# Rows for the maxima cleared ahead of a group's transfers, value sums behind the hash bits, and six lists of a hand-written order

## The chip, the core and the metric

The program runs on one core of a Trainium2 chip. TensorE (PE) multiplies, VectorE (DVE), ScalarE (ACT) and GpSimd (POOL) work element by element, and SyncE (SP) issues most of the transfers. Each engine takes its own instructions strictly in order and waits on semaphores for the others. The metric is the time of one launch in microseconds (us); lower is better.

## What is computed

Inputs are q, k and v of 4 batches, 8 heads, 768 rows of 64, and a projection of 64 to 6. Attention is masked by hash buckets, and a routed two-layer network follows (its part is not touched here and is cut):

```
q_bits = (einsum('bhsd,dk->bhsk', q, proj) > 0);  k_bits likewise
mask   = q_bucket[:, :, :, None] == k_bucket[:, :, None, :]
scores = where(mask, scale * q @ k.T, -1e9)
attn   = exp(scores - max);  attn = attn / (sum(attn) + 1e-9)
x      = attn @ v, heads side by side      # 3072 tokens of 512
out    = the token's expert: relu(x @ w1[e]) @ w2[e]
```

## The kernel before

The 32 heads are worked in 8 groups G of 4 heads (j = 0 to 3). Each group's operands lie in tiles QA, KA, QB, KB, VH, VL, WF, of which there are two copies, taken in turn (u = G%2). The partitions of QA are shared out: 0 to 63 hold q in half precision, 64 to 69 the six signs of its hash bits, and 96 to 127 a row block for the negated row maximum, which must be zero while the maximum itself is being found.

Time in the program is counted in steps t, six to a head (one for each 128 keys), and in half-steps n = 2t and 2t+1. In step t of head h, PE makes two halves of the scores transposed (`ST`, L258 and L259, each into one of three PSUM tiles `pst`), one score block for the maximum of a head up to nine steps ahead (`S_pass`, L240, into `pss`), and the products with the values four steps behind (`AV`, L273 to L275, closed by L279 or L280). ACT takes the exponential of each half (L260, `pt`). The rounding rest of `pt`, called `lo` (L263), is made by POOL, or by DVE for the steps named in `XL` and `PAT`: `XL` lists for a head the steps that DVE takes, and a head that is not listed has `PAT`, [5] for an even one and [3] for an odd one (heads 0 and 1 have lists of their own). DVE also reduces each `pss` (L242) to the maximum and divides the finished head by its sum (`norm`, L287 to L290). Heads end as pairs in the transfer to `x_dram` (L293).

A group is prepared while the group ahead of it is worked. All of that is placed by hand: a function is put down for a half-step with `add`, and the tables `P1`, `P2`, `P3` (groups 1 to 3) and `P4` (the later ones, counted from 48(G-1)) give the half-steps. Entries 0 to 7 are the casts of q and k to half precision on ACT (`cast`, L128), 8 to 11 their rests on POOL (`sub`, L130), 12 the hash bits (`bits`: 16 matmuls of 32 columns on PE, L142, a compare on DVE, L143; `bscale` one half-step later), 15 the casts of the values (`cv`, L192) with their rests on POOL (`sv`, L193), and 18 `sumv`: twelve matmuls of 32 columns (L204) that add up the values and a copy to `sq` (L206), followed SW = 4 half-steps later by `sumw` (two matmuls L210, a cast L213, and a DVE instruction L214 that writes WF).

`moves(G)`, at half-step MV, puts the group's operands in place: 22 transfers on SP's queue in one row, among them the rows of qa, qb, ka, kb (L174 to L180), the eight transfers of signs (L172, 9 KB each), and the loads of the next group's q and k (L61, 768 KB each). `clear(G)`, at half-step 48(G-1)+CL, is one transfer of zeros, 192 KB, to partitions 96 to 127 of QA (L191). For group 2, `moves` stands at half-step 59, and `clear` also at 59 (48+11); it is added later and so comes behind it. For the groups behind it, `moves` stands at 96 or 48(G-1)+1, and `clear` ten or eleven half-steps later.

Of the kernel before, what the change touches and what calls it, by code (L numbers as in the profile page):

```python
# [19 lines left out]
AP=dict(PAT=[[5], [3]],  # L20
 E0=[3, 5],
 E1=[3, 4],
 X=[2, 2, 5],
 MR=2,
 LEAD=9,
 S=[7, 7],
 DW=[12, 0, 0, 0, 384],
 P1=[13, 13, 14, 16, 17, 17, 23, 21, 16, 27, 21, 26, 23, 24, 33, 32, 3, 4, 49, -7, 3, 13],
 P2=[41, 44, 48, 49, 51, 51, 57, 55, 45, 49, 55, 57, 52, 60, 59, 61, 2, 3, 75, 32, 36, 47],
 P3=[69, 74, 83, 83, 85, 87, 88, 86, 77, 83, 87, 89, 94, 95, 96, 106, 0, 1, 120, 59, 63, 88],  # L30
 P4=[-33, -34, -25, -21, -13, -5, -9, -5, -18, -12, -3, 0, -5, 7, 10, 10, 3, 4, 36, -55, -50, -11],
 L0=[109, 2],
 EA=[[0, 0], [0, -1], [307, 4]],
 SW=4,
 XL={4: [0, 3, 5], 7: [1], 8: [0, 2, 4], 12: [2, 4, 5], 14: [0, 5], 18: [0, 5], 20: [0, 5], 29: [0, 1, 5], 30: [2]},
 BS=1,
 MV=[27, 59, 96, 1],
 CL=11,
 WS=-23,
 SU=16,  # L40
 OPS='b0 i3 i2 t0 w2 b1 w3 r0 r2 s0 w2 s1 C1 C0 r1 t1 c1 w4 s2 c0 w3 g0 l0 l1 u0 u1 B0 m0 a0 D0 s3 L0 L1 w2 e0 s4 d0 r3 l3 v2 v0 e1 w2 s5 e2 r5 l2 m1 s6 | s7 | x0 | s8 | v1 x1 | s9 | r4 s10 m2 | | s11 v3 f0 | x3 | | x2 m3 | | | | | |')
# [4 lines left out]
def attention(tc, nc, ctx, qT, kT, vv, proj, wg, x_dram, L, jp, identf, B, late=None, after=None):  # L46
# [84 lines left out]
    def bits(G,pairs):  # L131
        if (G,'b') not in TMP: TMP[G,'b']=dp.tile([128,S],F16,name="bt",bufs=1)
        bt=TMP[G,'b']; r=slice(0,128)
        ps=psS.tile([128,2,512],F32,name="pss")
        for hf in range(2):
            if G==0:
                for w in range(2):
                    T.matmul(ps[32*w:32*w+32,hf,0:384],pr,(qd,kd)[w][:,1,hf*384:hf*384+384],start=True,stop=True,tile_position=(0,32*w))
            for p in pairs:
                for w in range(2):  # L140
                    cg=64*p+32*w
                    T.matmul(ps[cg:cg+32,hf,0:384],pr,LD[G][w][:,p,hf*384:hf*384+384],start=True,stop=True,tile_position=(0,cg))  # L142
        V.tensor_scalar(bt.rearrange("p (z q) -> p z q",z=2),ps[:,:,0:384],0.0,0.5,op0=ALU.is_gt,op1=ALU.subtract)  # L143
# [51 lines left out]
    def sumv(G):  # L195
        u=G%2
        if G<2:
            A.copy(WF[u][96:128,:,64],wc[96:128,:].to_broadcast([32,4]))
        ps=psT.tile([128,512],F32,name="pst")
        n=0  # L200
        for c in range(6):
            for src in (VH[u],VL[u]):
                g=32*(n%4)
                T.matmul(ps[g:g+32,0:256].rearrange("p (j d) -> p j d",j=4),on,src[:,:,c,0:64],start=n<4,stop=n>7,skip_group_check=True,tile_position=(0,g)); n+=1  # L204
        SQ[G]=dp.tile([128,256],F32,name="sq",bufs=1)
        A.copy(SQ[G],ps[:,0:256])  # L206
# [54 lines left out]
    def lo(h,kc,eng):  # L261
        p,l=PT[h,kc]
        eng.tensor_tensor(l,p,p.bitcast(BF)[:,1::2],op=ALU.subtract)  # L263
# [18 lines left out]
    def norm(h):  # L282
# [8 lines left out]
        if hh%2:  # L291
            r=slice(64*hh-64,64*hh+64)
            SY.dma_start(x_dram[b*768:(b+1)*768,r].rearrange("(c p) d -> p c d",p=128),X[b][:,:,r])  # L293
    XH,XL=(XT[:,2*i:2*i+2].bitcast(F16).rearrange("p d c q -> p (d c q)").rearrange("p (d c q) -> p d c q",d=4,c=6) for i in range(2))
    def wsplit():
        A.copy(wgs[:,:,0],wgr); G_.tensor_tensor(wgs[:,:,1],wgr,wgs[:,:,0],op=ALU.subtract)
    def xtr(b,d,hf):
# [3 lines left out]
        A.copy(XH[:,d,r],p)  # L301
        V.tensor_tensor(XL[:,d,r],p,XH[:,d,r],op=ALU.subtract)
    LP=[]
    def logits(b,ds):
# [3 lines left out]
        for d in ds:  # L308
            for c in range(6): T.matmul(p[:,c],XH[:,d,c],wgs[:,d],start=(d==0 and c==0),stop=False,skip_group_check=True)
            for c in range(6): T.matmul(p[:,c,0],XL[:,d,c],wgs[:,d,0],start=False,stop=(d==3 and c==5),skip_group_check=True)  # L310
        if ds[-1]==3: V.reduce_sum(L[:,b*6:b*6+6],p.rearrange("p c z e -> p c e z"),axis=AX.X)
# [3 lines left out]
    def add(n,f,*a): at.setdefault(n,[]).append((f,a))  # L315
# [10 lines left out]
    for o in AP['OPS'].split():  # L326
# [2 lines left out]
        else: add(n,OPS[o[0]],int(o[1:]))  # L329
        if o[0]=='e': early.append(int(o[1:]))  # L330
    add(AP['WS'],wsplit); add(AP['SU'],sumv,0); add(AP['SU']+2,sumw,0)
    for G in range(1,NG):
        p=AP['P1'] if G==1 else AP['P2'] if G==2 else AP['P3'] if G==3 else [48*(G-1)+x for x in AP['P4']]
        st,sg=(AP['P4'] if G>3 else p)[16:18]
        for w in range(3):
            if w==2: add(p[19+w],load,G,w)
        for n in range(8): add(p[n],cast,G,n//2%2,n//4,n%2)
        for n in range(4): add(p[8+n],sub,G,n%2,n//2)
        add(p[12],bits,G,[0,1]); add(p[12]+AP['BS'],bscale,G); add(AP['MV'][G-1] if G<4 else 48*(G-1)+AP['MV'][3],moves,G)
        for j in range(4): add(p[15]+st*j,cv,G,j); add(p[15]+st*j+sg,sv,G,j,G_)  # L340
        add(p[18],sumv,G); add(p[18]+AP['SW'],sumw,G)
        if G>1: add(48*(G-1)+AP['CL'],clear,G)

    k=12; done={}; half={}; S_at={}
# [18 lines left out]
    def run(n):  # L363
        for f,a in at.get(n,[]): f(*a)
# [5 lines left out]
    for t in range(6*NH+LAG+6):  # L370
# [7 lines left out]
        if t>=1 and (t-1)//6<NH:  # L378
            hh,ss=divmod(t-1,6)
            lo(hh,ss,V if ss in (E0 if hh<1 else E1 if hh<2 else AP['XL'].get(hh,PAT[hh%2])) or t==6*NH else G_)  # L380
        run(2*t+1)
# [540 lines left out]
@with_exitstack  # L922
def tile_bucket_attention_moe(ctx, tc, qT, kT, vv, proj, wg, w1, w2, out):
    nc = tc.nc
    B = qT.shape[0] // 2
    drp = ctx.enter_context(tc.tile_pool(name="drp", bufs=1, space=DR))
    x_dram = drp.tile([768 * B, 512], F32, name="x_dram")
    M = Moe(tc, nc, ctx, 768 * B)
    late = M.consts()
    with ExitStack() as c1:  # L930
        c1.enter_context(tc.manual_schedule())
        attention(tc, nc, c1, qT, kT, vv, proj, wg, x_dram, M.Lm, M.jp, M.identf, B, late, M.early)
    with ExitStack() as c2:
        M.open(c2, x_dram, w1, w2, out)
        with tc.manual_schedule():
            M.start()
            M.run()
# [34 lines left out]
```

## Time and profile before

| | us |
|---|---|
| median of three runs | 703.8 (703.52 to 705.65) |
| the profiled execution | 706.58 |
| its span in the trace | 704.4 |
| PE busy in the span | 664.3 (94%) |
| POOL, DVE, ACT busy | 517.8, 499.9, 472.1 |

Attention fills the span to about 380 us, the routed network the rest. PE counts as busy from the start of a matmul to its modelled end, so that a stretch with short gaps shows as full; the clock (PEclk) is the share of TensorE's 2.4 GHz that was granted, and 0.50 is its lower level, 1.2 GHz. An "idle before" in square brackets behind a row of the timeline is how long the engine had nothing to do ahead of it, and what released it; "issue" means that the profile shows no engine that did.

### The profile page before, as it was taken

Reading aid. Unit: us, or ns where it says so; the run is one execution under the profiler, and the core shown is the slowest. Engines: PE = TensorE matmul, PEld = TensorE weight load, DVE = VectorE, ACT = ScalarE, POOL = GpSimd, SP = SyncE. Lnnn points to the kernel's source line nnn. Section 1 sums busy time; section 2 is a strip of 40 time slices with the busy share of each in tenths; the row PEclk is TensorE's granted clock in tenths of the full one; section 3 lists DMA queues with packets and bytes.
Section 4 is the critical chain, followed back from the end, with each engine's and each line's share of the span. In section 5 each row is a group of like instructions: output and inputs, shape, how many; then the busy total and the mean of one; then the engine's idle time right before and its main releaser. Section 6 shows DMA issues by size and latency. Waiting matters only on the chain. (4 is left out here: it accounts for less than half of the span.)

```text
span 704.4 us, 19362 instructions
## 1 busy us (share of the span) xinstructions
PE 664.3 (94%) x7952; PEld 434.9 (62%) x7952; DVE 499.9 (71%) x1118; ACT 472.1 (67%) x886; POOL 517.8 (74%) x457
## 2 busy tenths in 40 slices
PE   8899979999999999999998589999999999999995
PEld 3566756776767767677766485555555555555552
DVE  6769848787977888878884678777787887834120
ACT  8878847787887878876764055756565656575840
POOL 7999978898898989988654256575766665677851
PEclk9999989999999999999999589999999999999998
DMA  9746842826537355350000171726262626363601
GB/s 225 206 116 183 193 139 52 211 71 139 145 100 189 95 140 154 98 118 24 24 25 26 49 237 21 282 76 251 88 242 86 244 82 233 98 247 104 227 29 45
DMA packets 39951, 93.58 MB, mean 133 GB/s; under 512 B 4548, under 2 KB 30520, under 8 KB 37816
## 3 DMA queue, kind: packets, MB, share of 16 engines
q1 hardware_dynamic: 33048, 46.21, 25.1%
q0 software_dynamic: 6816, 46.15, 18.5%
q8 instruction: 62, 1.02, 0.6%
q14 instruction: 25, 0.20, 0.1%
HBM read 59.53 MB, written 12.58 MB: 102 GB/s over the span
## 5 line engine op out<-in xcount | busy, mean ns | idle before, releaser
L263 POOL TENSOR_TENSOR lo<-pt 128x768 f16<-128x768 f32 x148 | 228.1, 1555 | 39.3 <-ACT pt L260 38.0
L260 ACT ACTIVATE pt<-pst 128x384 f32<-128x384 f32 x384 | 181.7, 491 | 64.1 <-PE pst L259 52.5
L242 DVE TENSOR_REDUCE m<-pss 128x1 f16<-128x770 f32 x192 | 181.1, 956 | 42.8 <-PE pss L240 42.1
L258 PE MATMUL pst<-qa,ka 128*128 128x384 f16 x384 | 125.7, 327 | 4.0 <-ACT qa L249 2.3
L259 PE MATMUL pst<-qb,kb 128*128 128x384 f16 x384 | 125.4, 327 | 0.0
L273 PE MATMUL psv<-vh,pt 128*128 128x65 f16 x1152 | 121.0, 195 | 1.1 <-DVE X L290 1.1
L274 PE MATMUL psv<-vl,pt 128*128 128x64 f16 x1152 | 121.1, 193 | 0.0
L275 PE MATMUL psv<-vh,lo 128*128 128x65 f16 x1152 | 121.1, 194 | 0.0
L273 PEld LDWEIGHTS <-pt 128*128 128x128 bf16 x1152 | 106.9, 98 | 9.1 <-issue 1.0
L274 PEld LDWEIGHTS <-pt 128*128 128x128 bf16 x1152 | 105.8, 99 | 9.5 <-issue 1.7
L275 PEld LDWEIGHTS <-lo 128*128 128x128 f16 x1152 | 106.0, 98 | 0.0
L240 PE MATMUL pss<-ka,qa 128*128 128x385 f16 x384 | 94.7, 330 | 6.4 <-issue 4.7
L782 POOL TENSOR_TENSOR wl<-wf,wh 128x512 f16<-128x512 f32 x72 | 82.7, 1172 | 21.7 <-ACT wf L773 21.2
L764 ACT ACTIVATE wh<-wf 128x1024 f16<-128x1024 f32 x64 | 67.0, 1051 | 35.6 <-PE psa L732 20.8
L842 PEld LDWEIGHTS <-wh 128*128 128x128 f16 x480 | 45.3, 97 | 30.0 <-issue 1.1
L854 PEld LDWEIGHTS <-hh 128*128 128x128 f16 x384 | 35.8, 97 | 38.6 <-issue 0.8
L773 ACT ACTIVATE wf<-wf 128x1024 f32<-128x1024 f32 x55 | 57.8, 1054 | 0.9
L240 PEld LDWEIGHTS <-qa 128*128 128x128 f16 x384 | 37.1, 97 | 32.4 <-issue 5.7
L263 DVE TENSOR_TENSOR lo<-pt 128x768 f16<-128x768 f32 x44 | 55.3, 1257 | 1.8 <-ACT pt L260 1.8
L857 ACT ACTIVATE o<-po 128x512 f32<-128x512 f32 x24 | 14.3, 595 | 62.5 <-PE po L854 51.9
L747 POOL DMA_INDIRECT xg<-x_dram,zidx x24 | 24.0, 1002 | 38.9 <-DVE zbnd L701 28.5
L755 POOL DMA_INDIRECT wf<-in_w_dram,zwidx x20 | 22.8, 1140 | 36.7 <-DVE zmi L688 20.6
(282 smaller groups left out, 1378.5 us busy)
## 6 DMA issues: line engine op xcount, KB each, us to landing
vp<-in_vv_dram SPq DMA_DIRECT2D x8, 768.0 KB
x_dram<-X SPq DMA_DIRECT2D x16, 384.0 KB
qp<-in_qT_dram SPq DMA_DIRECT2D x7, 768.0 KB
kp<-in_kT_dram SPq DMA_DIRECT2D x7, 768.0 KB
qa<-qh SPq DMA_DIRECT2D x14, 192.0 KB
qb<-qh SPq DMA_DIRECT2D x14, 192.0 KB
ka<-kh SPq DMA_DIRECT2D x14, 192.0 KB
kb<-kh SPq DMA_DIRECT2D x14, 192.0 KB
```

The costliest lines, as they stand in the source:

```text
L240: T.matmul(ps[:,hf,0:HK],QA[u][:,j,qc*128:qc*128+128],KA[u][:,j,hf*HK:hf*HK+HK],start=True,stop=True)
L242: V.tensor_reduce(M6[h][:,qc:qc+1],ps[:,:,0:HK],axis=AX.XY,op=ALU.max,negate=True)
L258: T.matmul(ps[:,0:384],KA[u][:,j,kr],QA[u][:,j,r],start=True,stop=False)
L259: T.matmul(ps[:,0:384],KB[u][:,j,kr],QB[u][:,j,r],start=False,stop=True)
L260: A.activation(PT[h,kc][0][:,r],ps[:,0:384],AF.Exp,scale=0.125)
L263: eng.tensor_tensor(l,p,p.bitcast(BF)[:,1::2],op=ALU.subtract)
L273: T.matmul(av[:,c,:],ph[:,r],VH[u][:,j,kc,:],start=(kc==0 and c==0),stop=False,skip_group_check=True)
L274: T.matmul(av[:,c,0:64],ph[:,r],VL[u][:,j,kc,:],start=False,stop=False,skip_group_check=True)
L275: T.matmul(av[:,c,:],l[:,r],VH[u][:,j,kc,:],start=False,stop=False,skip_group_check=True)
L764: s.nc.scalar.mul(h[:,r],f[:,r],WSC)
L773: s.nc.scalar.mul(f[:,r],f[:,r],WSC)
L782: for _ in range(n): s.nc.gpsimd.tensor_tensor(*s.pend.pop(0)[1],op=ALU.subtract)
```

## The change

Four things are done:

- CL is 9 instead of 11. `clear(2)` falls on half-step 57, ahead of `moves(2)` at 59. For the later groups nothing else stands on SP's queue between the two places.
- `sumv` of groups 1 to 6 leaves its own half-step (49, 75, 120, and 48(G-1)+36) and is called directly behind `bits` of the group that follows (`hash_sum`), at 52, 94, 139 and so on; `sumw` goes with it, four half-steps behind. Group 7 has none behind it and stays.
- `XL` gives DVE one more `lo` in each of heads 2, 6, 7 and 10 (step 0, and step 4 in head 7); head 8 has three as before, at steps 0, 3, 5 instead of 0, 2, 4.
- `P2[15]`, the casts of group 2's values, is 60 instead of 61.

```
- P2=[41, 44, 48, 49, 51, 51, 57, 55, 45, 49, 55, 57, 52, 60, 59, 61, 2, 3, 75, 32, 36, 47],
+ P2=[41, 44, 48, 49, 51, 51, 57, 55, 45, 49, 55, 57, 52, 60, 59, 60, 2, 3, 75, 32, 36, 47],
- XL={4: [0, 3, 5], 7: [1], 8: [0, 2, 4], 12: [2, 4, 5], ...
+ XL={2: [0, 5], 4: [0, 3, 5], 6: [0, 5], 7: [1, 4], 8: [0, 3, 5], 10: [0, 5], 12: [2, 4, 5], ...
- CL=11,
+ CL=9,
+    def slots(G): return AP['P1'] if G==1 else AP['P2'] if G==2 else AP['P3'] if G==3 else [48*(G-1)+x for x in AP['P4']]
+    def hash_sum(G):
+        bits(G,[0,1])
+        if G>1: sumv(G-1)
...
-        add(p[12],bits,G,[0,1]); add(p[12]+AP['BS'],bscale,G); ...
+        add(p[12],hash_sum,G); add(p[12]+AP['BS'],bscale,G); ...
-        add(p[18],sumv,G); add(p[18]+AP['SW'],sumw,G)
+        if G==NG-1: add(p[18],sumv,G)
+        add((slots(G+1)[12] if G<NG-1 else p[18])+AP['SW'],sumw,G)
         if G>1: add(48*(G-1)+AP['CL'],clear,G)
```

On SP's queue one row moves past 22 others. `qa_180` is the first copy of QA, which groups 0, 2, 4, 6 use; `wrm` is the tile of zeros:

```order
 L293 DMA x_dram<-X 128x6x128
+L191 DMA qa_180<-wrm 32x8x384
 L174 DMA qa_180<-qh 64x2x768 x2
 L176 DMA qb_182<-qh 64x2x768 x2
@@ -74,5 +75,4 @@
 L172 DMA ka_181<-bt 6x768
 L61 DMA kp<-in_kT_dram 128x1536
-L191 DMA qa_180<-wrm 32x8x384
 L293 DMA x_dram<-X 128x6x128
```

The clear stood behind all of `moves(2)`, its last row the 768 KB load `kp` of group 3; now it is the first of them, behind the transfer of the heads 2 and 3.

On PE, behind the hash bits of group 3 (head 7, step 5), the kernel before goes on with the scores of that step:

```order
L142 MATMUL pss<-qp,pr 32x384
L142 MATMUL pss<-kp,pr 32x384
L258 LDWEIGHTS ka_185
L258 MATMUL pst<-qa_184,ka_185 128x384
L259 LDWEIGHTS kb_187
```

The changed kernel has the value sums of group 2 between the two:

```order
L142 MATMUL pss<-qp,pr 32x384
L142 MATMUL pss<-kp,pr 32x384
L204 LDWEIGHTS on
L204 MATMUL pst<-vh_218,on 32x256
L204 LDWEIGHTS on
L204 MATMUL pst<-vl_219,on 32x256
```

The twelve L204 are the same; they have left head 6 (step 1), where they stood between two matmuls of 128 columns.

On POOL, in head 6 (`ql` is the rest of group 3's q, `vl` that of group 2's values), one `lo` is gone:

```order
 L263 TENSOR_TENSOR lo<-pt 128x768
 L193 TENSOR_TENSOR vl_219<-vp,vh_218 128x384 x2
-L263 TENSOR_TENSOR lo<-pt 128x768 x4
+L263 TENSOR_TENSOR lo<-pt 128x768 x3
 L130 TENSOR_TENSOR ql<-qp,qh 128x768
 L263 TENSOR_TENSOR lo<-pt 128x768 x3
```

DVE has it instead, between two of its reductions.

## Rows read from the trace of the kernel before

**Rows 1.** The page: busy us, share of the span, instructions.

```profile
PE 664.3 (94%) x7952; PEld 434.9 (62%) x7952; DVE 499.9 (71%) x1118; ACT 472.1 (67%) x886; POOL 517.8 (74%) x457
```

**Rows 2.** Stretches: busy us (xcount) of PE, PEld, DVE, ACT, POOL; clock; DMA share; GB/s.

```profile
93.70:98.80 5.10, 0.35 (x4) 0.04 (x2) 0.91 (x3) 0.49 (x1) 4.26 (x3) 0.90 1.04 329
98.80:104.60 5.80, 5.80 (x34) 3.91 (x35) 2.98 (x4) 2.98 (x6) 1.50 (x2) 0.50 0.17 66
104.60:120.00 15.40, 14.41 (x213) 9.85 (x211) 12.56 (x15) 11.26 (x25) 13.67 (x9) 1.00 0.09 19
```

**Rows 3.** Timeline of PE, head 6, steps 3 to 5: start, us, instruction.

```profile
93.71 0.33 PE L259 MATMUL pst<-qb,kb 128*128 128x384 f16 x1
98.79 0.80 PE L240 MATMUL pss<-ka,qa 128*128 128x385 f16 x2 [4.75 <-issue]
...
100.34 1.06 PE L210 MATMUL pst<-sq,onf 128*128 128x256 f32 x2
...
104.69 0.33 PE L258 MATMUL pst<-qa,ka 128*128 128x384 f16 x1
```

**Rows 4.** Timeline of SP's queue, 73 to 96 us.

```profile
73.31 0.38 SPq L293 DMA_DIRECT2D x_dram<-X  x1
74.21 1.31 SPq L174 DMA_DIRECT2D qa<-qh  x2
...
91.11 0.66 SPq L172 DMA_DIRECT2D ka<-bt  x1
91.87 0.38 SPq L61 DMA_DIRECT2D kp<-in_kT_dram  x1
92.36 0.72 SPq L191 DMA_DIRECT2D qa<-wrm  x1
```

**Rows 5.** The same steps of head 14 on PE.

```profile
190.75 0.49 PE L240 MATMUL pss<-ka,qa 128*128 128x385 f16 x2
...
193.61 0.33 PE L258 MATMUL pst<-qa,ka 128*128 128x384 f16 x1
```

**Rows 6.** Timeline of PE at group 4's hash bits, head 11.

```profile
159.52 0.33 PE L258 MATMUL pst<-qa,ka 128*128 128x384 f16 x1
159.68 0.33 PE L259 MATMUL pst<-qb,kb 128*128 128x384 f16 x1
159.93 0.51 PE L142 MATMUL pss<-qp,pr 128*32 128x384 f32 x1
...
160.93 0.48 PE L142 MATMUL pss<-qp,pr 128*32 128x384 f32 x1
...
161.36 0.34 PE L258 MATMUL pst<-qa,ka 128*128 128x384 f16 x1
```

**Rows 7.** All of `lo`, by engine: shortest, median, longest ns (40 to 200 us).

```profile
L263 POOL TENSOR_TENSOR lo<-pt x61: 1456/1464/2182, 41.1 to 199.8; 128x768 f16<-128x768 f32 x61
L263 DVE TENSOR_TENSOR lo<-pt x20: 945/1376/2091, 56.0 to 197.3; 128x768 f16<-128x768 f32 x20
```

**Rows 8.** Who waited for whom, 106 to 140 us: us, times, longest.

```profile
PE pst L258 <- ACT pt L260: 0.9, 1, 0.9
PEld pss L142 <- DVE m L242: 0.8, 1, 0.8
PE psv L273 <- DVE X L290: 0.6, 1, 0.6
```

**Rows 9.** Timeline of ACT: the first casts of group 3's k.

```profile
106.77 0.92 ACT L128 CAST kh<-kp 128x384 f16<-128x384 f32 x2
```

**Rows 10.** Timeline of POOL around the stand of PE.

```profile
96.51 1.46 POOL L263 TENSOR_TENSOR lo<-pt 128x768 f16<-128x768 f32 x1
101.27 1.47 POOL L263 TENSOR_TENSOR lo<-pt 128x768 f16<-128x768 f32 x1 [3.30 <-ACT pt L260]
```

**Rows 11.** Transfers: KB of one.

```profile
kp<-in_kT_dram SPq DMA_DIRECT2D x7, 768.0 KB
qa<-wrm SPq DMA_DIRECT2D x6, 192.0 KB
```

More of the change, by code (lines that the diff above doesn't have):

```diff
@@ L34 @@
  SW=4,
- XL={4: [0, 3, 5], 7: [1], 8: [0, 2, 4], 12: [2, 4, 5], 14: [0, 5], 18: [0, 5], 20: [0, 5], 29: [0, 1, 5], 30: [2]},
+ XL={2: [0, 5], 4: [0, 3, 5], 6: [0, 5], 7: [1, 4], 8: [0, 3, 5], 10: [0, 5], 12: [2, 4, 5], 14: [0, 5], 18: [0, 5], 20: [0, 5], 29: [0, 1, 5], 30: [2]},
  BS=1,
  MV=[27, 59, 96, 1],
- CL=11,
+ CL=9,
  WS=-23,
@@ L331, in attention @@
     add(AP['WS'],wsplit); add(AP['SU'],sumv,0); add(AP['SU']+2,sumw,0)
+    def slots(G): return AP['P1'] if G==1 else AP['P2'] if G==2 else AP['P3'] if G==3 else [48*(G-1)+x for x in AP['P4']]
+    def hash_sum(G):
+        bits(G,[0,1])
+        if G>1: sumv(G-1)
     for G in range(1,NG):
-        p=AP['P1'] if G==1 else AP['P2'] if G==2 else AP['P3'] if G==3 else [48*(G-1)+x for x in AP['P4']]
+        p=slots(G)
         st,sg=(AP['P4'] if G>3 else p)[16:18]
@@ L338, in attention @@
         for n in range(4): add(p[8+n],sub,G,n%2,n//2)
-        add(p[12],bits,G,[0,1]); add(p[12]+AP['BS'],bscale,G); add(AP['MV'][G-1] if G<4 else 48*(G-1)+AP['MV'][3],moves,G)
+        add(p[12],hash_sum,G); add(p[12]+AP['BS'],bscale,G); add(AP['MV'][G-1] if G<4 else 48*(G-1)+AP['MV'][3],moves,G)
         for j in range(4): add(p[15]+st*j,cv,G,j); add(p[15]+st*j+sg,sv,G,j,G_)
-        add(p[18],sumv,G); add(p[18]+AP['SW'],sumw,G)
+        if G==NG-1: add(p[18],sumv,G)
+        add((slots(G+1)[12] if G<NG-1 else p[18])+AP['SW'],sumw,G)
         if G>1: add(48*(G-1)+AP['CL'],clear,G)
```

## Prediction

> **What bounds the kernel now.** The page comes first: PE is busy for 664.3 us of a span of 704.4 and no other engine for more than 518 [rows 1], so an edit pays where PE stands still or is slowed, and hardly elsewhere. The view by stretches then shows the one large hole in the attention part. From 93.7 to 98.8 us PE is busy for 0.35 us of 5.10, and in the 5.8 us behind it the granted clock is 0.50, the lower level, with PE busy throughout [rows 2]. DVE (0.91) and ACT (0.49) stand too; only POOL (4.26) goes on, and the transfers run at 329 GB/s. So PE waits for a transfer.
>
> The timeline of PE says for which use: the last matmul ahead of the hole is an L259 at 93.71, the first behind it the L240 at 98.79, the score block `S_pass` of head 8, the first of group 2, which reads QA and KA; the releaser is "issue", no engine [rows 3]. The timeline of SP's queue shows what of QA is late. All 22 transfers of `moves(2)` stand ahead of the clear: qa at 74.21, the last sign at 91.11, then the load kp at 91.87, and only at 92.36 the clear [rows 4]. The load is 768 KB and the clear 192 KB [rows 11]; at 329 GB/s [rows 2] the two need about (0.79 + 0.20 MB) / 329 = 3.0 us, and they share the rate with the x_dram transfer that follows, so an end near 98.7 fits the clear. The signs of head 8, the first two of eight, went out some 5 us earlier.
>
> **The clear ahead of the transfers.** It now stands behind the x_dram transfer, whose issue at 73.31 [rows 4] already waits for head 3's `norm`, and that for the last product that reads rows 96 to 127 of group 0's QA; the clear's own wait is for that product and adds nothing. Nobody but SP's queue stands behind it. It takes SP 0.72 us there, of which the gap between 73.31 + 0.38 and 74.21 hides 0.5 [rows 4]: the transfers of `moves(2)` go out 0.2 to 0.8 us later. What waits for them first is the S_pass itself, at 93.9. The last sign at 91.11 plus 0.66 plus 0.8 is 92.6, and head 8 needs the first two only; I cost this at nothing, and up to 0.8 if that cover is gone.
>
> What goes is the stand: two matmuls of a step follow each other by 0.16 us (159.52 to 159.68 [rows 6]), so the L240 would have come at 93.87 instead of 98.79 [rows 3]: **4.9 us**. With it goes the slow clock behind it. From that L240 to the L258 of step 5 it takes 104.69 - 98.79 = 5.90 us [rows 3]; the same steps of head 14, at full clock, take 193.61 - 190.75 = 2.86 [rows 5]. Head 6 has two L210 more, 1.06 us at half clock [rows 3], so 0.53 at full. That leaves 5.90 - 2.86 - 0.53 = **2.5 us** lost to the clock: PE was fully busy in that stretch, at 0.50 [rows 2], after 4.9 us without a matmul.
>
> What is late next? POOL's `lo` is the candidate, as its queue is longest there: it ended its last one ahead of the hole's end at 97.97 and then waited 3.30 us for ACT [rows 10], that is, the stand is where POOL caught up. Without the stand, step 5 of head 6 begins at 93.87 + 2.86 = 96.7 [rows 5], and the `lo` that ended at 97.97, that of step 2, is used one step later, at 96.7 + 1.4 = 98.1 or behind it (half of 2.86 for a step); one `lo` ahead of it has moved to DVE, which brings its end to 96.5. I cost it at nothing.
>
> **The value sums behind the hash bits.** No instruction is added. Each run of 32-column matmuls costs PE a change on either side: L259 to L142 takes 0.25 us where 0.16 is the spacing, and from the last L142 to the next L258 0.43, where a round of L142 takes (160.93 - 159.93) / 3 = 0.33 [rows 6]: 0.09 and 0.10. With two runs placed together, two of four changes drop out, 0.2 us a group. No row shows an L142 with an L204 behind it. If the change from 32-bit to 16-bit operands costs as much, nothing is won; if none, six groups win 6 x 0.2 = 1.2 us. I take **0.9**, nearer to the upper end, since both lines have the tile shape 128*32 [rows 6]. Behind the sums are queued the second half of that step's scores and ACT's exponential, which get 0.35 us more to wait in that step and as much less in the one that the sums have left; `sumw` and WF are needed ten half-steps or more later and are hidden.
>
> The page "TensorEngine Tiling (Array Packing)" of the Trainium skill, under Key Properties, says that a change of the tiling mode, not merely of the tile, drains TensorE. By that the step from L142 to L204 would cost nothing and the term would be 1.2 instead of 0.9; no run here shows it.
>
> **The moved `lo`.** Four go from POOL, at 1.46 us each, to DVE, at 0.95 to 2.09 [rows 7], and one of head 8's three comes a step later. In heads 7 to 9 PE has three waits: 0.8 us for DVE's reduction ahead of the bits, 0.6 for `norm`, 0.9 for ACT [rows 8]. DVE is already busy for 12.56 of 15.40 us there [rows 2] and gets one more `lo` in each of heads 6 and 7. From below: the waits vanish, -1.2 (half of the 2.3). From above: one more `lo` of 2.09 stands ahead of a reduction that PE waits for, +2.1. I take **+0.4**, since DVE's longer list lies nearer than POOL's relief. P2[15] moves four casts by half a step where ACT has room: nothing.
>
> The page "GPSIMD Engine Reference" of the Trainium skill, under Specifications, speaks against this part: GpSimd shares its SBUF interface with VectorE and contends with VectorE's instructions of two SBUF inputs, which `lo` is. The spread of 945 to 2091 ns on DVE and 1456 to 2182 on POOL [rows 7] agrees. By it in full each moved `lo` would cost DVE 2.09 us and the sum would take the upper end, +2.1 instead of +0.4.
>
> **The sum.** -4.9 - 2.5 - 0.9 + 0.4 = -7.9 us, on a span of 704.4 and an execution of 706.58: 698.7. The median of the runs, 703.8, lies 2.8 under that execution. The terms are stretches of PE and do not scale with that, so I take them from the median: **695.9**. What lies behind attention waits for its end and moves as a whole.
>
> **The rivals.**
>
> *New waits eat part of it.* With the stand gone, ACT, DVE and POOL have no stretch in which to catch up. The three waits of heads 7 to 9 [rows 8], 2.3 us together, double, and the upper end of the moved `lo` is added to it: -7.9 + 2.3 + 1.7 = -3.9, 699.9. For it speaks DVE's share of 12.56 in 15.40 [rows 2]; against it that DVE and ACT stood idle, not behind, when PE stopped. Chance 0.14.
>
> *It doesn't do what it says.* What the S_pass waits for is not the clear but another transfer of `moves(2)` that ends at the same time. Then the stand stays, and only the sums' 0.9 is won: 702.9. Against it: the last of those left SP at 91.11, 2.7 us ahead of the stand. Chance 0.05.
>
> *Slower: group 3's k becomes the late thing.* ACT's casts L128 of that k stand at half-step 83, in order ahead of the next exponentials. They ran at 106.77 [rows 9], and all of that comes 7.4 us earlier, at about 99.4, while the load kp goes out at 91.87 as before or up to 0.8 us later [rows 4]. If it has not landed, ACT waits, PE runs out of `pst` tiles and stands, and the clock falls again. In the kernel before, kp goes ahead of the clear, so by my estimate it landed at about 96.5. To cost more than 7.9 us it would have to land later than 99.4 + 7.9 = 107.3, some 11 us later than that; then a time of 704 to 707. From 99.4 on it costs something, from 107.3 on it decides. Chance 0.04.
>
> **How the numbers follow.** The forecast has 0.77, the rivals 0.14, 0.05 and 0.04. The lower end: 703.8 - 4.9 - 2.5 - 1.2 - 1.2 = 694.0, less 0.3 for the spread of the runs: 693.7. The upper end: -4.9 - 2.5 - 0 + 2.1 gives 698.5; to take in the first rival it reaches to 699.9. A measurement of this kernel can tell some 0.3%, 2.1 us, from no change: the forecast and the first rival are faster, 0.91; the second rival is no change, 0.05; the third slower, 0.04.
>
> **What would show it.** The stretch between the last score block of group 1 and the first of group 2 on PE: no idle time above 1 us, and no clock of 0.50 in attention. On SP's queue, L191 between L293 and the first L174 of group 2. An L204 within 0.35 us behind the last L142. Heads 7 to 9 on DVE: the waits of [rows 8] each under 1.5 us. The prediction is wrong if L240 of head 8 still waits for "issue", if ACT's casts at half-step 83 wait for a DMA, or if PE's waits for DVE grow by more than 2 us.

## The result, and the profile after

The changed kernel takes 696.11 us (median of six runs, 695.03 to 698.35) where the kernel before, timed beside it, takes 703.66 (702.01 to 706.63): a ratio of 0.9892, with a 95% interval of 0.9866 to 0.9917. It is 7.6 us faster; 695.9 had been predicted. Its profiled execution took 697.58 us with a span of 695.8, against 706.58 and 704.4 before.

The page of the changed kernel, with the same columns as [rows 1]: PE is busy 3.7 us less; DVE has 3.3 us more and POOL 2.0 less, as four `lo` have moved from one to the other.

```profile
PE 660.6 (95%) x7952; PEld 435.5 (63%) x7952; DVE 503.2 (72%) x1122; ACT 472.3 (68%) x886; POOL 515.8 (74%) x453
```

The timeline of PE in head 6, steps 3 to 5, answers [rows 3].

```profile
93.53 0.32 PE L259 MATMUL pst<-qb,kb 128*128 128x384 f16 x1
93.69 0.49 PE L240 MATMUL pss<-ka,qa 128*128 128x385 f16 x2
...
96.56 0.33 PE L258 MATMUL pst<-qa,ka 128*128 128x384 f16 x1
```

The score block of head 8 now follows the L259 by 0.16 us; it followed by 5.08. From that L240 to the L258 of step 5 it takes 96.56 - 93.69 = 2.87 us where it took 5.90. Stretches of the changed kernel, with the columns of [rows 2]; the first is these three steps, the other three are head 9:

```profile
93.37:98.41 5.04, 5.04 (x70) 3.63 (x66) 4.57 (x9) 3.95 (x9) 5.04 (x4) 1.00 0.97 301
121.74:125.35 3.61, 2.67 (x65) 2.01 (x62) 3.61 (x5) 3.25 (x8) 3.61 (x4) 1.00 0.52 133
125.35:128.76 3.41, 3.41 (x40) 2.38 (x37) 1.58 (x3) 1.38 (x3) 3.32 (x3) 0.50 1.03 263
128.76:135.43 6.67, 6.67 (x116) 5.08 (x114) 4.91 (x8) 4.75 (x11) 5.25 (x7) 1.00 0.45 123
```

In head 6 PE is full at a clock of 1.00 while the transfers run at 301 GB/s (329 in the stand [rows 2]): they move as before, and PE no longer waits for them. But head 9 has a stretch of 3.41 us at 0.50, the lower level, that the kernel before did not have there. What stands ahead of it on PE is one wait of 0.94 us, and then the narrow matmuls of the router's logits:

```profile
123.50 0.32 PE L258 MATMUL pst<-qa,ka 128*128 128x384 f16 x1 [0.94 <-ACT pt L260]
...
124.09 0.30 PE L309 MATMUL pst<-wgs,XT 128*128 128x16 f16 x6
124.24 0.29 PE L310 MATMUL pst<-wgs,XT 128*128 128x8 f16 x6
```

ACT is late there because the four casts of group 3's values stand in one row, at 120.93, for 1.75 us. The kernel before has such a wait there too (0.9 [rows 8]), without the lower clock behind it. The timeline of ACT, with the first cast of group 3's k that answers [rows 9], now without a wait:

```profile
98.64 0.93 ACT L128 CAST kh<-kp 128x384 f16<-128x384 f32 x2
...
120.93 1.75 ACT L192 CAST vh<-vp 128x384 f16<-128x384 f32 x4
```

SP's queue of the changed kernel, against [rows 4]. The clear stands behind the x_dram transfer. Counted from the span's start qa goes out 0.31 us later than before, the last sign 0.64 later, the load kp 0.59 later; but head 6 itself starts 0.58 later here (87.89 against 87.31), and counted from its start the load leaves at 4.57 us where it left at 4.56.

```profile
72.82 0.38 SPq L293 DMA_DIRECT2D x_dram<-X  x1
73.71 0.71 SPq L191 DMA_DIRECT2D qa<-wrm  x1
74.52 1.28 SPq L174 DMA_DIRECT2D qa<-qh  x2
...
91.75 0.66 SPq L172 DMA_DIRECT2D ka<-bt  x1
92.46 0.44 SPq L61 DMA_DIRECT2D kp<-in_kT_dram  x1
```

PE at group 4's hash bits, against [rows 6]. A round of L142 begins every 0.32 to 0.34 us, and the first L204 comes 0.32 behind the start of the last round: the step from one to the other costs nothing that these rows can show.

```profile
152.67 0.51 PE L142 MATMUL pss<-qp,pr 128*32 128x384 f32 x1
...
153.66 0.49 PE L142 MATMUL pss<-qp,pr 128*32 128x384 f32 x1
...
153.98 0.27 PE L204 MATMUL pst<-vh,on 128*32 128x256 f16 x1
...
154.44 0.34 PE L258 MATMUL pst<-qa,ka 128*128 128x384 f16 x1
```

From the first L142 to the next L258 it is 1.77 us where it was 1.43, so the twelve sums cost 0.34 here; the step that they have left lost 0.55 (step 1 of head 6: 2.09 to 1.54). That is 0.21 us for a group, put together from two places. And `lo` by engine, against [rows 7]:

```profile
L263 POOL TENSOR_TENSOR lo<-pt x60: 1457/1468/2259, 41.4 to 199.9; 128x768 f16<-128x768 f32 x60
L263 DVE TENSOR_TENSOR lo<-pt x25: 945/1136/2278, 46.4 to 199.3; 128x768 f16<-128x768 f32 x25
```

Head by head the two profiles can be laid beside each other, from the L258 that opens a head to the one that opens the next. Where nothing differs these lengths agree to 0.03 us, which is far finer than the medians of the runs; so all that follows is read from them first. (One exception: in the two runs with the clear between, heads 19 and 24 are 0.12 and 0.28 us shorter than in the changed kernel, with no edit there and no row that says why.) "2 to 31" is from the start of head 2 to that of head 31.

| us | head 6 | 7 | 8 | 9 | 10 and 11 | 12 to 31 | 2 to 31 |
|---|---|---|---|---|---|---|---|
| before | 19.23 | 12.43 | 10.86 | 11.88 | 22.72 | 206.08 | 327.79 |
| before, second profile | 19.66 | 12.43 | 10.87 | 11.88 | 22.71 | 206.08 | 328.21 |
| changed | 10.52 | 11.75 | 11.58 | 13.69 | 22.50 | 205.81 | 320.72 |
| changed, second profile | 10.51 | 11.76 | 11.58 | 12.07 | 22.49 | 205.76 | 319.03 |
| clear alone | 12.19 | 12.71 | 10.88 | 11.88 | 22.71 | 206.12 | 321.07 |
| clear ahead of kp only | 13.14 | 12.45 | 10.88 | 11.88 | 22.71 | 206.11 | 321.76 |
| sums alone | 14.74 | 12.77 | 12.61 | 11.21 | 22.61 | 205.76 | 324.23 |
| all but the clear | 15.08 | 12.77 | 11.57 | 12.08 | 22.49 | 205.77 | 324.56 |
| lists alone | 19.17 | 12.44 | 10.72 | 11.99 | 22.72 | 206.10 | 328.00 |
| changed, old lists | 10.53 | 13.28 | 12.61 | 11.21 | 22.62 | 205.55 | 320.75 |
| the same, second profile | 10.51 | 12.46 | 12.62 | 11.21 | 22.63 | 205.58 | 319.97 |
| changed, casts spread | 10.51 | 11.77 | 11.58 | 13.70 | 22.49 | 205.78 | 320.99 |
| clear between | 10.52 | 11.75 | 11.58 | 12.08 | 22.49 | 205.39 | 318.66 |
| clear between, early casts | 10.52 | 11.76 | 12.21 | 11.03 | 22.49 | 205.40 | 318.27 |

### The profile page after: what moved, and what is told of

The parts are those of the page before. It is cut to its first block, busy times and chain, and to the rows that moved or that the text cites. A ratio compares the mean times of both kernels' runs of the same rounds, so it can differ in the third digit from the quotient of the medians.

```text
span 695.8 us, 19356 instructions
## 1 busy us (share of the span) xinstructions
PE 660.6 (95%) x7952; PEld 435.5 (63%) x7952; DVE 503.2 (72%) x1122; ACT 472.3 (68%) x886; POOL 515.8 (74%) x453
## 5 line engine op out<-in xcount | busy, mean ns | idle before, releaser
L263 POOL TENSOR_TENSOR lo<-pt 128x768 f16<-128x768 f32 x144 | 224.2, 1571 | 40.8 <-ACT pt L260 38.1
L258 PE MATMUL pst<-qa,ka 128*128 128x384 f16 x384 | 125.4, 327 | 4.6 <-ACT qa L249 2.6
L259 PE MATMUL pst<-qb,kb 128*128 128x384 f16 x384 | 125.2, 326 | 0.0
L240 PE MATMUL pss<-ka,qa 128*128 128x385 f16 x384 | 94.4, 329 | 1.7 <-DMA ka<-bt 1.1
L263 DVE TENSOR_TENSOR lo<-pt 128x768 f16<-128x768 f32 x48 | 60.1, 1253 | 1.9 <-ACT pt L260 1.8
L240 PEld LDWEIGHTS <-qa 128*128 128x128 f16 x384 | 37.2, 97 | 27.4 <-issue 1.5
```

What stands on the lines that cost most here:

```text
L240: T.matmul(ps[:,hf,0:HK],QA[u][:,j,qc*128:qc*128+128],KA[u][:,j,hf*HK:hf*HK+HK],start=True,stop=True)
L258: T.matmul(ps[:,0:384],KA[u][:,j,kr],QA[u][:,j,r],start=True,stop=False)
L259: T.matmul(ps[:,0:384],KB[u][:,j,kr],QB[u][:,j,r],start=False,stop=True)
```

## The experiments

### The clear alone, and all but the clear

The kernel before with one number changed:

```
- CL=11,
+ CL=9,
```

> The kernel before with CL = 9 alone: the clear of group 2 goes ahead of that group's transfers, the sums, the lists and P2 stay. Theory (the stand of PE in head 6 and the slow clock behind it come from the clear): head 6 falls from 19.2 us to about 11.0 (the 10.5 of the changed kernel and the 0.44 of the value sums, which stay in it), and the ratio to the kernel before is that of a gain of 6.5 to 7.5 us (0.990). Rival (another transfer of the same row is what PE waits for): head 6 keeps a stand of 4 to 5 us, ratio 1.000. Open besides: whether head 9 grows from 11.9 us as it does in the changed kernel (13.7, with a clock of 0.50 in it). If that comes from the stand being gone, it is here too; if it comes from the new lists, head 9 stays at 11.9 to 12.1.

Measured: 697.37 us (median of four runs), a ratio of 0.9914, interval 0.9887 to 0.9941. Head 6 is 12.19 us. Its timeline of PE:

```profile
93.18 0.33 PE L259 MATMUL pst<-qb,kb 128*128 128x384 f16 x1
93.34 0.49 PE L240 MATMUL pss<-ka,qa 128*128 128x385 f16 x2
```

The stand is gone by this one number, and with it the slow clock: head 6 loses 7.04 us. I had expected 11.0 for it; steps 1 and 3, which still hold the sums and `sumw`, are 0.55 and 0.68 us above those of the changed kernel, steps 0 and 4 0.2 each. The runs gain 6.0 us (703.39 beside it), where 6.5 to 7.5 had been expected. Head 9 keeps its 11.88, so the clear alone does not lengthen it. A new thing shows on ACT:

```profile
100.78 0.92 ACT L128 CAST kh<-kp 128x384 f16<-128x384 f32 x2 [1.62 <-DMA kp<-in_kT_dram]
```

The load kp left SP only at 94.61 in this execution, 7.84 us behind the start of head 6 (4.56 before), the cast waited 1.62 us for it, and step 0 of head 7 took 3.19 us instead of 1.69. That is the third rival, at 1.6 us. SP's waits, 70 to 100 us, show where the load was held up. By the profile the last transfer of the rests (L185) waits for the landing of the load qp, eight rows ahead of it on the queue; it reads nothing of qp, and why it needs that landing no row says. Before:

```profile
SPq L185 <- DMA qp<-in_qT_dram: 1.6, 1, 1.6
```

and with the clear alone, where one of the signs (L172) waits too:

```profile
SPq L185 <- DMA qp<-in_qT_dram: 2.8, 1, 2.8
SPq L172 <- DMA qb<-ql: 1.3, 1, 1.3
```

The other half, the changed kernel with the number set back (`CL=11`):

> The changed kernel with CL = 11 again: the clear of group 2 stands behind that group's transfers as before, the merged sums, the lists and P2 as changed. Theory: the stand is back, head 6 at 18.5 to 19.2 us, and what is left is the sums' gain of 0.5 to 0.9 us, ratio 0.999. Rival (the clear alone isn't the cause; the lists or the sums removed the stand): head 6 at 10.5 to 11, ratio 0.990. If head 9 keeps its 13.7 us with a clock of 0.50 here, the new lists make it; at 11.9 it takes both.

Measured: 701.67 us (nine runs), ratio 0.9978, interval 0.9963 to 0.9993. The stand is there, shorter:

```profile
96.51 0.49 PE L240 MATMUL pss<-ka,qa 128*128 128x385 f16 x2 [2.97 <-DMA kp<-in_kT_dram]
```

The row names the load kp, which is ahead of the clear on the queue; but with the clear alone PE went on at 93.34, before kp had left SP at 94.61, so kp is not what PE needs. The clear is what removes the stand; sums and lists don't. But head 6 is 15.08, not 18.5 to 19.2: the stand is 2.97 us instead of 4.75, and the clock behind it is 0.50 for 3.41 us instead of 6.83. Head 9 is 12.08.

### The clear ahead of the load only

The kernel before; group 2's clear is issued behind the signs and ahead of the load of the next group's k:

```
-        elif G==2: qa(); qb(); nxt(0); ka(); kb(); low(); signs(); nxt(1)
+        elif G==2: qa(); qb(); nxt(0); ka(); kb(); low(); signs(); clear(2); nxt(1)
...
-        if G>1: add(48*(G-1)+AP['CL'],clear,G)
+        if G>2: add(48*(G-1)+AP['CL'],clear,G)
```

> The kernel before with the clear of group 2 issued inside that group's transfers: behind the last transfer of the signs and ahead of the 768 KB load of the next group's k. It is still behind 20 of the 22 rows that the change moves it past. Theory A (it is the load's bytes ahead of it that make it late): the clear goes out at about 91.9 us instead of 92.4, lands at about 94 to 95, and the stand shrinks from 4.75 us to 0 to 1.5; head 6 at 11 to 13 us. Theory B (a transfer of zeros to 32 partitions is slow by itself, some 6 us from issue to landing, load or no load): the stand shrinks only by the 0.5 us of the earlier issue, to about 4.3, head 6 at 18.5. Ratio 0.990 to 0.993 by A, 0.999 by B.

Measured: 697.99 us (six runs), ratio 0.9941, interval 0.9911 to 0.9970. SP's queue:

```profile
92.62 0.72 SPq L191 DMA_DIRECT2D qa<-wrm  x1
93.39 0.60 SPq L61 DMA_DIRECT2D kp<-in_kT_dram  x1
```

and PE:

```profile
95.69 0.50 PE L240 MATMUL pss<-ka,qa 128*128 128x385 f16 x2 [0.85 <-DMA qa<-wrm]
```

This is the plainest row of the study. The clear left 0.26 us later than before (92.62 against 92.36), and PE could go on 3.1 us earlier (95.69 against 98.79): from its issue to PE's start it took 3.07 us with the load behind it, and 98.79 - 92.36 = 6.43 with the load ahead of it. The trace now names the releaser as the clear itself, where [rows 3] had only "issue". Theory A holds, though the ratio is that of a smaller gain than its 0.990 to 0.993; the interval reaches into that range. One place on the queue was worth 19.23 - 13.14 = 6.1 of the 7.0 us that head 6 lost with the clear ahead of everything.

### The sums alone

`hash_sum` and the move of `sumw`, as in the diff of the change, in the kernel before; clear, lists and P2 stay.

> The kernel before with the value sums of groups 1 to 6 behind the next group's hash bits, and nothing else. Theory: two changes of the matmul's width fewer in each of six groups, 0.2 us each, so the heads of a pair of places shrink by 0.2 us together and attention by 0.9 to 1.3 us; ratio 0.999. Rival (the step from a 32-bit matmul to a 16-bit one costs as much as the changes saved): attention equal within 0.2 us. The stand in head 6 stays either way, at 4.5 to 5 us.

Measured: 701.65 us (ten runs), ratio 0.9973, interval 0.9961 to 0.9986. The gain of 0.2 us a group is there in part: 22.72 to 22.61 in heads 10 and 11 (one group), 206.08 to 205.76 in heads 12 to 31 (three). Heads 15 and 23 are 0.22 shorter each and head 19 by 0.09, while head 20 is 0.20 longer with no row that says why. What I had not expected is the stand:

```profile
95.57 0.49 PE L240 MATMUL pss<-ka,qa 128*128 128x385 f16 x2 [2.46 <-DMA kp<-in_kT_dram]
```

2.46 us and not 4.75; head 6 is 4.5 us shorter. In this execution the clear left at 90.37, 3.39 us behind the start of head 6 where it had been 5.05, and landed in time to let PE go 5.20 us later instead of 6.43. Of those 1.66 us, 0.59 are there at the first row of the queue (qa leaves 13.69 us ahead of head 6, 13.10 before); SP's wait of 1.6 us for the load qp is absent besides, and other rows of the queue took some 0.5 longer. The profiled execution was the fastest of the ten, though, and the median moved by 2 us only, so 2.46 is likely the short end. In this and the run with all but the clear, the two profiles with the sums moved, the stand is 2.5 and 3.0; in the three without, 4.75, 4.86 and 5.96. That the sums shorten it fits these five; but with all but the clear SP's wait for qp is back, at 1.0 us. The runs allow less of it: by the interval they are 1.0 to 2.7 us faster, where this profile has heads 2 to 31 shorter by 3.56. How much of the shorter stand is the program's stays open.

### The lists alone, and the changed kernel with the old lists

First the kernel before with the lists and P2[15] of the change (five lists differ, those of heads 2, 6, 7, 8 and 10; the title and the expectations say six):

> The kernel before with the six lists and P2[15] alone; the clear and the sums stay. Theory (the lists move no wait on which PE's end hangs, +0.4 by the prediction, and the stand stays): head 6 at 18.5 to 19.2 us, heads 2 to 10 together within 0.6 us of before, ratio 1.000. Rival (the lists bring group 2's transfers out earlier, as the merged sums alone did, and so shorten the stand by 2 us): head 6 at 15 to 17 us, ratio 0.996. Rival from above (each moved one costs DVE 2.09 us in front of a reduction): heads 7 to 9 longer by 2 us, ratio 1.003.

Measured: 700.61 us (ten runs), ratio 0.9961, interval 0.9939 to 0.9984, while its profile shows nothing of a gain: heads 2 to 31 take 328.00, the stand is 4.86.

```profile
99.34 0.80 PE L240 MATMUL pss<-ka,qa 128*128 128x385 f16 x2 [4.86 <-issue]
```

The profiled execution took 703.94 us and was one of the two slowest of the ten; what the other eight gained has left no trace. Heads 7 to 9 take 35.15 us, 35.17 before, so the rival from above fell, and head 6 at 19.17 speaks against the other. Inconclusive on the whole: the rows say nothing is won, the runs say some 3 us.

Then the changed kernel with the lists of before, twice:

```
- XL={2: [0, 5], 4: [0, 3, 5], 6: [0, 5], 7: [1, 4], 8: [0, 3, 5], 10: [0, 5], 12: [2, 4, 5], ...
+ XL={4: [0, 3, 5], 7: [1], 8: [0, 2, 4], 12: [2, 4, 5], ...
```

> The changed kernel with the six lists of the kernel before; the clear, the sums and P2[15] as changed. It tells what the lists are worth once the stand is gone. Theory A (the lists are needed: with the clear alone, the last signs of group 2 and so the load kp went out 2 us later, ACT's casts of group 3's k waited 1.6 us for it and head 7's step 0 took 3.19 us instead of 1.69): here too, head 7 at 12.8 or more, attention 1 us longer than in the changed kernel. Theory B (the late load comes from that execution's transfers and not from the lists): head 7 at 11.7 to 12, attention as in the changed kernel within 0.3 us. And if the lists make head 9's wait and the clock of 0.50 there, head 9 is 11.9 here and attention 1 to 1.8 us shorter.

> The changed kernel with the old lists once more, for a second profile. With the old lists and the clear moved, in two profiles of two, ACT's cast of group 3's k waited 1.6 and 1.8 us for the load kp and head 7's step 0 took 3.2 and 3.4 us; with the new lists, in three of three, there was no such wait and 1.69 us. Theory (the lists bring the load in time): the wait of 1.6 to 1.9 us is here again, head 7 at 13.2. Rival (it hangs on the execution's transfers): no wait, head 7 at 11.7 to 12.5.

Measured: 695.54 us (four runs), ratio 0.9888, interval 0.9855 to 0.9920; the second profile took 695.85. The first has ACT's wait for the load:

```profile
100.64 0.92 ACT L128 CAST kh<-kp 128x384 f16<-128x384 f32 x2 [1.83 <-DMA kp<-in_kT_dram]
```

and the second, of the same program, has not:

```profile
98.41 0.92 ACT L128 CAST kh<-kp 128x384 f16<-128x384 f32 x2
```

Head 7 is 13.28 in the one and 12.46 in the other. In the first, PE stands behind ACT's late casts:

```profile
102.00 0.32 PE L258 MATMUL pst<-qa,ka 128*128 128x384 f16 x1 [1.55 <-ACT pt L260]
```

SP's wait for the load qp is 3.5 us in the first and 2.3 in the second. So the late load hangs on how the transfers of an execution land, and the theory that it comes whenever the lists are old fell. That the new lists make it rarer isn't excluded: with the clear ahead of all, it came in two of three executions with the old lists and in none of three with the new. Against the changed kernel without its slow stretch (319.03), the second profile (319.97) puts the lists at a gain of 0.9 us: heads 7 to 9 take 36.29 with the old and 35.41 with the new. Of that 0.70 is in head 7, where PE waits twice for DVE with the old lists, and with the new ones not at all:

```profile
106.26 0.19 PE L273 MATMUL psv<-vh,pt 128*128 128x65 f16 x1 [0.29 <-DVE X L290]
...
108.00 0.51 PE L142 MATMUL pss<-qp,pr 128*32 128x384 f32 x1 [0.38 <-DVE m L242]
```

The medians, 695.54 and 696.11, don't show the gain.

### The changed kernel again, and its casts spread

> The changed kernel once more, unaltered, for a second profile of it. Theory (what its first profile shows is of the program, since head times of one program agree to 0.1 us elsewhere): head 9 at 13.7 us with a clock of 0.50 for 3.4 us in it, the load kp out at about 92.5 us. Rival (the clock of 0.50 in head 9 hangs on the execution): head 9 at 12 to 12.6 us with the full clock, head 31 some 1.2 to 1.7 us earlier.

Measured: 694.03 us, and a second profile in which head 9 takes 12.07 us instead of 13.69. PE's wait ahead of it is the same to the hundredth:

```profile
122.92 0.32 PE L258 MATMUL pst<-qa,ka 128*128 128x384 f16 x1 [0.94 <-ACT pt L260]
```

and the clock of the whole head is 1.00:

```profile
121.16:133.23 12.07, 11.13 (x210) 8.50 (x207) 10.08 (x15) 9.08 (x21) 11.82 (x13) 1.00 0.68 183
```

From head 2 on, all other heads agree within 0.03 us. So the stretch at half clock belongs to the execution, and it costs 13.69 - 12.07 = 1.62 us when it comes. Three other kernels have the same wait there, at 0.93 to 0.94 us (the lists alone, all but the clear, the clear between), and in their profiles the clock of head 9 is 1.00. The other experiment tried to take its supposed cause away:

```
- P3=[..., 94, 95, 96, 106, 0, 1, 120, 59, 63, 88],
+ P3=[..., 94, 95, 96, 106, 1, 1, 120, 59, 63, 88],
```

> The changed kernel with P3[16] = 1 instead of 0: ACT's four casts of group 3's values stand one half-step apart instead of all on one. In the changed kernel they run in one row of 1.75 us from 120.93 us, PE waits 0.94 us for the exponential behind them, and the granted clock is 0.50 from 125.35 to 128.76. Theory (that row makes the wait, and the wait the clock): no wait over 0.4 us, no clock of 0.50 in heads 8 to 10, head 9 at 11.0 to 11.9 instead of 13.7, ratio to the kernel before 0.986 to 0.988. Rival (the clock falls for the narrow matmuls of the logits, which PE has in that step anyway): the wait goes, the clock of 0.50 stays, head 9 at 12.7 to 13, ratio 0.989.

Measured: 696.43 us (six runs), ratio 0.9899, interval 0.9868 to 0.9929. The wait for ACT went, and another came, for DVE's copy `XT` of the logits' input, which PE's transposes need:

```profile
124.48 0.33 PE L248 MATMUL pst<-ident,m 128*128 128x128 f16 x3 [1.04 <-DVE XT L302]
```

The clock fell behind it as in the first profile of the changed kernel:

```profile
126.39:129.80 3.41, 3.41 (x32) 2.18 (x29) 1.08 (x2) 1.89 (x4) 3.33 (x4) 0.50 1.04 260
```

Neither the theory nor the rival was put to the test, since a wait of the same size stayed.

### The clear between, and early casts

The changed kernel; the clear goes out behind the eight transfers of q, k and their rests, ahead of the signs (`low(); clear(2); signs()`), and no longer at half-step 57.

> The changed kernel with one transfer in another place: the clear of group 2 goes out behind the eight transfers of q, k and their rests and ahead of the signs, instead of ahead of all. In the runs with the clear ahead of all, the first sign left at -1.8 to +0.5 us from the start of head 6 and the load kp at +4.6 to +7.8; with the clear behind, at -3.2 to -1.7 and +2.9 to +4.6. Theory (the clear's 192 KB delay what stands behind it on the queue, and the stand needs it only to land by +5.9): no stand in head 6 (10.5 us), kp out at +4 to +5, head 7 11.8 us, no wait of ACT's casts for kp; ratio as the changed kernel, 0.988 to 0.990. Rival (behind the row of eight it lands as late as behind the signs): a stand of 0.9 us or more, head 6 at 11.5 to 13, ratio 0.992 to 0.994.

Measured: 696.46 us (six runs), ratio 0.9896, interval 0.9878 to 0.9915. SP's queue:

```profile
86.19 0.69 SPq L191 DMA_DIRECT2D qa<-wrm  x1
86.93 0.81 SPq L172 DMA_DIRECT2D qa<-bt  x1
...
92.96 0.44 SPq L61 DMA_DIRECT2D kp<-in_kT_dram  x1
```

and PE, whose score block of head 8 follows the L259 by 0.16 us:

```profile
93.65 0.32 PE L259 MATMUL pst<-qb,kb 128*128 128x384 f16 x1
93.81 0.49 PE L240 MATMUL pss<-ka,qa 128*128 128x385 f16 x2
```

No stand: the rival fell. The clear may thus stand in either of these two places ahead of the signs. But the load left no earlier for it, 4.95 us behind the start of head 6, where the changed kernel had 4.57 and 5.52; that the clear's bytes delay what is behind it isn't borne out.

To this the early casts were added (`106, 0, 1` in P3 becomes `103, 1, 1`):

> The kernel of the run with the clear between, and P3[15] = 103, P3[16] = 1: the four casts of group 3's values one half-step apart, from half-step 103 to 106, instead of all on 106. Spread to 106 to 109 they left PE a wait of 1.04 us for DVE's XT in place of 0.94 for ACT's exponential. Theory (three half-steps earlier they delay neither): head 9's step 0 at 3.1 to 3.6 us instead of 4.1 to 4.5, no clock of 0.50 in head 9, ratio 0.986 to 0.988. Rival (ACT's casts then delay the exponentials of head 8 instead): head 8 grows from 11.6 by 0.5 to 1 us, ratio as the changed kernel's, 0.989.

Measured: 694.60 us (four runs), ratio 0.9863, interval 0.9842 to 0.9884, the lowest median of the study. Stretches of heads 8 and 9:

```profile
110.29:122.50 12.21, 11.52 (x170) 8.37 (x167) 11.20 (x14) 9.77 (x22) 8.94 (x7) 1.00 0.75 185
122.50:133.53 11.03, 11.03 (x211) 8.49 (x208) 8.86 (x14) 8.09 (x18) 10.78 (x12) 1.00 0.73 199
```

Theory and rival are each half right. PE has no idle time in head 9, which falls from 12.08 to 11.03, step 0 from 4.09 to 3.03; head 8 grows from 11.58 to 12.21. Together 0.4 us are won by the heads, and the clock is 1.00 in both heads. The median lies 1.5 us under that of the changed kernel; since the intervals of the ratios overlap (0.9842 to 0.9884 and 0.9866 to 0.9917), I don't call it shown that it is faster than the change.

### The kernel before again

> The kernel before once more, for a second profile of it. Its first profile has a stand of 4.75 us and a clock of 0.50 for 6.83 us, in an execution 2.9 us above the median; with the sums or with sums and lists changed, the stand was 2.5 and 3.0 us and the clock 0.50 for 3.41. Theory (the length of the stand hangs on how soon the transfers of that execution land, so the first profile overstates it for the median): a stand of 2.5 to 4 us, head 6 at 15 to 18 us, a time of 701 to 704. Rival (the stand is of the program, and it was the moved sums that shortened it): 4.75 within 0.2, head 6 at 19.2 within 0.2.

Measured: 703.21 us, and:

```profile
99.73 0.80 PE L240 MATMUL pss<-ka,qa 128*128 128x385 f16 x2 [5.96 <-DMA kp<-in_kT_dram]
```

The stand is 5.96 us here and the time near the median all the same; the theory that the first profile overstated it fell, and so did the rival's 4.75 within 0.2. In both profiles the clock was 0.50 for 6.83 us.

## Why the prediction was right, and where it was not

**The stand, 4.9 us, and the clock behind it, 2.5.** Right, and the greatest part of the result. With the clear alone, head 6 lost 7.04 us where 7.4 had been summed up, and with all but the clear the stand was there. In the runs the clear alone gives 6.0 of the 7.6 us; that the other edits add to it is not shown by them, as the intervals of the ratios overlap (0.9887 to 0.9941 and 0.9866 to 0.9917). The reading that it was the last transfer, 192 KB behind 768, came from four rows of SP's queue [rows 4] and was shown by the run with the clear ahead of the load only. One sum in it does not come out: 3.0 us from 92.36 end at 95.4 and not near 98.7, and PE went on 6.43 us behind the clear's issue. The transfer to x_dram and the load vp, 384 and 768 KB, left SP at 94.76 and 95.25; the four together, 2.16 MB, would take 6.6 us from 91.87 at 329 GB/s, to 98.4. That is an estimate, and no run tests it. The second profile of before gives 5.96 for the stand, so the term itself scatters by a microsecond with the landing of the transfers.

**The clear in its new place, nothing.** With the clear alone, qa left SP 1.70 us behind the x_dram transfer (72.77 to 74.47) where it had been 0.90 [rows 4]: 0.8 later, the upper end, so the gap that was to hide 0.5 hid nothing. In the changed kernel it doesn't show, because there the x_dram transfer leaves 15.07 us ahead of head 6 instead of 14.00. PE waits for none of these transfers. **POOL's `lo` not late:** right, no row of head 6 waits for one.

**The sums, -0.9.** This term was too large: with the clear moved, the sums are worth 0.3 us (321.07 to 320.75, both with the wait for the load). The 1.1 us to the second profile (319.97) also hold the end of that wait. The price of a change was right where it can be read, 0.21 us for a group, the upper end. What failed is taking it six times. The rule of the Trainium skill, page "TensorEngine Tiling (Array Packing)", Key Properties, by which the step would cost nothing, agrees with the 0.32 us from the last round of L142 to the first L204 (rounds at 0.32 to 0.34). In the profile of the sums alone, heads 15 and 23 gain 0.22 each, heads 10 and 11 0.11, heads 4 and 5 0.04, and heads 19 and 20 lose 0.11 together. That the sums might also shorten the stand was not seen; in the changed kernel that has no effect, since there the stand is gone.

**The lists, +0.4.** Here the step failed: I took DVE's longer list to weigh more than POOL's relief. With the stand gone the heads show the other sign, -0.9 (319.97 to 319.03), within the lower bound of -1.2; in the kernel before, the lists alone cost 0.2 (327.79 to 328.00), and the waits of [rows 8] stayed. The longest `lo` did grow, to 2259 ns on POOL and 2278 on DVE, but DVE's is 2256 with the old lists too, and DVE's median fell from 1376 to 1136. No wait came of it: the weight load's wait for DVE's reduction ahead of the bits is 0.5 us where it was 0.8 [rows 8], and PE's two waits of head 7, still 0.29 and 0.38 us with the old lists, are gone. The spread of 945 to 2278 ns agrees with the rule of the Trainium skill, page "GPSIMD Engine Reference", Specifications; the upper end of +2.1 that was put to it did not come. Two of head 8's three `lo` come a step later, not one, and P2[15] was in no run by itself, so that its nothing is not shown.

**The sum.** -7.04 - 0.3 - 0.9 is -8.2, and the two profiles of the changed kernel against the first of before give -7.07 and -8.76, by whether head 9 has the slow stretch. The forecast was -7.9, the medians -7.6. That the forecast came so near is in part luck: the sums gave 0.6 less than was put down for them and the lists 1.3 more. The executions as wholes differ by 9.0 us (706.58 to 697.58) and by 9.2 (703.21 to 694.03, the second profiles); what lies outside heads 2 to 31 is 376.6 and 372.9 us in the two spans of before and 375.1 and 373.2 in those of the changed kernel, so the median is where a sum of stretches is to be laid on, not a profiled time.

**"No clock of 0.50 in attention."** Wrong in one profile of two. I had tied the lower clock to a long stand; it also came behind a wait of 0.94 us and narrow matmuls, and it stayed away behind the same ones.

**The rivals.** New waits: heads 8 to 11 grew from 45.46 us to 46.14 without the slow stretch, 0.43 of that being `sumw`, which has moved into head 8 (step 1: 1.52 to 1.95). Of the three waits of [rows 8] two fell and one stayed at 0.9; none doubled. The list of waits of the changed kernel, 93 to 140 us:

```profile
PE pst L258 <- ACT pt L260: 0.9, 1, 0.9
...
PEld pss L142 <- DVE m L242: 0.5, 1, 0.5
```

The second rival fell with the first experiment. The third, the late load, was a real mechanism that I had put too far away: by the estimate 2.9 us lay between landing and cast (96.5 and 99.4), yet it cost two executions of other kernels 1.6 and 1.8 us of ACT's time. The estimate let the load leave as before or up to 0.8 us later; SP's wait for the load qp, which moves it by more than that, was not in it. The two profiles of the changed kernel passed it; the load left 4.57 and 5.52 us behind the start of head 6, where it cost something at 6.66 and 7.84. It never came near the 7.9 that it needed to turn the sign.

## What to carry to other kernels

When PE waits for "issue" and the rates of the transfers are high, read the queue backwards from the stand: a small transfer that is needed next, issued behind a large one that is needed later, can cost the large one's time (here 6.43 us until PE went on instead of 3.07), and the swap of the two rows cost nothing. Before adding up gains from one profile, ask which of them hang on the landing of transfers; those scatter by microseconds, while the lengths of nearly all heads elsewhere repeat to hundredths and are the better measure of a small edit. A gain that is read at one place of a row of like places is to be read at the others too before it is multiplied: the 0.2 us a group was there in full for two groups of six.

## What the runs showed of the hardware

- The clock's lower level comes behind short waits too, and not each time. Behind stands of 4.75, 4.86 and 5.96 us it held for 6.83 us, behind 2.46 and 2.97 for 3.41, behind 0.85 (the clear ahead of kp) not at all. Behind waits for ACT of 1.34 and 1.55 us in head 7 (the clear alone, the old lists) it didn't come either. Behind a wait of 0.94 us with narrow matmuls after it, it held for 3.41 us in one execution and not at all in another of the same program, nor in three other kernels with that wait; behind one of 1.04 us (casts spread) it held for 3.41. What decides that is open.
- A 192 KB transfer of zeros took 3.07 us from its issue to the start of the matmul that waited for it, and 5.2 to 7.2 us where a 768 KB load had left 0.5 us ahead of it.
- On SP's queue a 192 KB transfer waited for the landing of a 768 KB load eight rows ahead of it: 1.6 us in the kernel before, 2.8 and 3.5 us where the next load then came too late, not at all with the sums alone.
- On PE a step from 32-bit to 16-bit matmuls of the same tile shape, 128*32, cost nothing that the rows can show (0.32 us from the last round to the next run, rounds at 0.32 to 0.34); a step from 128*128 to 128*32 and back cost 0.09 and 0.10 us [rows 6].
